# Half of the bonus moved to GpSimd, and the experts' up matmuls widened to 464 columns with the second sum added behind them

## The chip, the cores and the metric

The kernel runs on one core of a Trainium2 chip. The metric is the device time of one execution in microseconds (us), as the median of several runs; less is better. Engines are named as in the profile: PE is TensorE (matmuls; PEld its weight loads), DVE is VectorE, ACT is ScalarE, POOL is GpSimd, SP is SyncE, which issues most DMAs.

## The reference

Two stages follow each other. The first is a linear attention with decay over 4 batches, 8 heads, 768 positions and 48 dimensions:

```python
for t in range(S):
    cur = np.einsum('bhd,bhe->bhde', u[None] * kt, vt)
    y[:, :, t] = np.einsum('bhd,bhde->bhe', rt, state + cur)
    state = w[None, :, :, None] * state + np.einsum('bhd,bhe->bhde', kt, vt)
```

The term with `u` is called the bonus here: position t sees its own key and value with the weight u. The second stage takes the 3072 rows of 384 numbers as tokens. A token whose `x @ w_skip` is positive goes to the one of 8 experts with the largest gate logit and gets

```python
h = np.maximum(xc[mask] @ w1[e], 0.0)
y[mask] = gate_w[mask, None] * (h @ w2[e])
```

added to itself; w1 is 384 x 1024 and w2 1024 x 384 for each expert. All is float32.

## The kernel before

**Attention.** The positions are cut into chunks of 64, and two batches are worked at a time, so there are NT = 24 steps. A step on TensorE is: the scores of the next chunk (L446), the part that comes from the state (`across`, L532), transposes of k (L459) and of an earlier output (L575), the state's update (L479) and the part within the chunk (`within`, L508), which needs the masked scores. VectorE masks the scores from PSUM with two COPY_PREDICATED (L467, L468); the next `within` waits for them. For the chunks to come, VectorE scales r by the decay (`prep_r`, part 0, L416) and multiplies half of the result by u (`prep_r`, part 1, L424: the first BH = 2 of 4 pairs of heads); ScalarE does the other half (`bonus`, L410). Both halves land in the tile `rd`, which the scores read. GpSimd scales k (`prep_k`, L434, tile `kd`). `rd` and `kd` have four buffers each.

The order of the work is written out by hand: each engine runs its instructions in the order of the program, and the loop over n (L893 to L936) lays them down. In step n come the scores, masks and `across` of chunk n + 1, the bonus half of chunk n + 2 on ScalarE, the transpose of k for n + 2, k for n + 3 on GpSimd, a slice of the routing on VectorE (`tick`, how many slices by the table DEAL), then `prep_r` of n + 3 in two parts with the state's update between them. From step 7 on, in twelve steps (LOADS with LEAD), GpSimd also splits a piece of expert 0's weights (L116), after ScalarE has rounded it (L115). Routing begins at step 8.

**Experts.** The kernel splits each float32 operand of the experts in a high part, rounded to the type float32r, and the rest. ScalarE makes the high part (`hi`, `xh`, `hh`), VectorE or GpSimd the low one (`lo`, `xl`, `hl`), and a product is the sum of three matmuls: high by high, high by low, low by high. Each expert has two tiles of tokens, 128 and 104 of CAP = 232. Experts 1 to 7 go through `expert`; expert 0, and expert 1's beginning, are interleaved by the string PLAN with `single`, which works on one tile of 128 tokens. For each of the 8 blocks of 128 features, `up` issues 9 matmuls of 232 columns: three chunks of w1 by (high by xh, high by xl, low by xh), each with a weight load of its own. Two blocks share one PSUM bank (464 columns), and `rectify` takes both at once: ScalarE writes hh = max(ph, 0), VectorE writes hl = max(ph, 0) − hh, both from PSUM. Four banks take turns. Then, per pair of blocks, two pieces of the next expert's weights are split (`split_next(2)`). There are 12 pieces of 128 x 512 an expert; those with j % 3 == 2 go to GpSimd (j % 6 == 2 for expert 2's pieces), the others to VectorE. Each split frees a buffer for the load of a piece of the expert after; NST2 = 14 buffers hold pieces on their way. After the ups, the next expert's tokens are transposed (`turn`), and the downs of the two tiles follow (L170, 24 matmuls of 384 columns each), which read hh and hl block by block. VectorE adds the result to the token (`mix`, L175) when a tile's downs are through, and GpSimd scatters it (L178).

At the start of expert 2 VectorE has six small checks (L1069 to L1075) ahead of its first rectify, at that of expert 3 six more (L1081 to L1086). Expert 7 has no weights to split.

Of the kernel before, what the change touches and what calls it, by code (L numbers as in the profile page):

```python
# [22 lines left out]
P = 128  # L23
# [7 lines left out]
CAP = 232  # L31
# [16 lines left out]
PLAN = "aaasBsaBBxBasBxsgaBBgusBgsBguBBgBs"  # L48
NPC = 12
NST = 4  # L50
NST2 = 14
LEAD = 3
LOADS = [4, 5, 6, 8, 9, 10, 12, 13, 14, 16, 17, 18, 19, 20, 21]
W_MIN, W_MAX = 0.8, 1.2
# [7 lines left out]
def tile_wkv_moe(  # L62
# [89 lines left out]
        nc.scalar.copy(xh, pt)  # L152
        nc.vector.tensor_tensor(xl, pt, xh.bitcast(F32), ALU.subtract)

    def up(ph, w1, f, xh, xl):
        fs = slice(f * P, (f + 1) * P)
        k = 0
        for c in range(NCC):
            for a, b in ((w1[0], xh), (w1[0], xl), (w1[1], xh)):
                nc.tensor.matmul(ph, a[:, c, fs], b[:, c, :], start=(k == 0), stop=(k == 3 * NCC - 1))  # L160
                k += 1

    def rectify(ph, hh, hl):
        nc.scalar.activation(hh, ph, AF.Relu)  # L164
        nc.vector.scalar_tensor_tensor(hl, ph, 0.0, hh.bitcast(F32), ALU.max, ALU.subtract)

    def down(py, w2, f, hh, hl):
        k = 3 * f
# [81 lines left out]
    with ExitStack() as actx:  # L250
# [158 lines left out]
                rd = rds[n][:, hp]  # L409
                nc.scalar.mul(rd[:, :, 1], rd[:, :, 0], uw[:, hp : hp + 1])  # L410

        def prep_r(n, parts=(0, 1)):
            d = loaded[n][0]
            if 0 in parts:
                rds[n] = wk.tile([DR, NHP, 2, 2, C], F32, tag="rd", name=f"rd{n}", bufs=4)
                nc.vector.tensor_tensor(  # L416
                    rds[n][:, :, :, 0],
                    d[:, 0],
                    w_d[:, n % NSUB, 0][:, :, None].to_broadcast([DR, NHP, 2, C]),
                    ALU.mult,  # L420
                )
            if 1 in parts:
                rd = rds[n]
                nc.vector.tensor_tensor(  # L424
                    rd[:, :BH, :, 1],
                    rd[:, :BH, :, 0],
                    uw[:, :BH, None, None].to_broadcast([DR, BH, 2, C]),
                    ALU.mult,
                )
# [463 lines left out]
        for n in range(NT - 1):  # L893
            if n + 5 < NT:
                load_dm(n + 5)
            if n + 4 < NT and n:
                load_v(n + 4)
            if n in LOADS:
                piece(LOADS.index(n))
            scores(n + 1)  # L900
            mask_scores(n + 1)
            across(n + 1)
            if n - LEAD in LOADS[:NPC]:
                piece(LOADS.index(n - LEAD), split=True)
            elif n == NT - 2:
                piece(NPC, split=True)
            if 0 < n and n + 2 < NT:
                bonus(n + 2, BH)
            turn_k(n + 2)
            if 0 < n <= TE and n % GB == 0:  # L910
                gate_back(n - 1)
            turn_x(n)
            if n + 3 < NT:
                prep_k(n + 3)
            for kind in (1, 2, 4):
                step_route(kind)
            tick(DEAL.get(n, 0))
            if n + 3 < NT:
                prep_r(n + 3, (0,))
            back = state(n + 1)  # L920
            if n + 3 < NT:
                prep_r(n + 3, (1,))
            if n == NT - 2:
                gate_some(n, NT - 1 - TE)
                while next(mid) == 0:
                    pass
            within(n + 1, kcopy.get(n + 2, xcopy[n]))
            evac(n + 1)
            if n < TE and n % GB == GB - 1:
                gate_some(n)  # L930
            if back:
                back()
            if n + 1 in ends:
                routes.append([route(ends[n + 1], n + 1), 0, n + 1])
            if 1 <= n < 5:
                next(setup, None)  # L936
# [31 lines left out]
    with ExitStack() as mctx:  # L968
# [12 lines left out]
        def splitter(e, skip=0):  # L981
            pieces = iter(range(skip, NPC) if e < E else ())

            def split_next(k):
                for _ in range(k):
                    j = next(pieces, None)
                    if j is not None:
                        split_piece(e, j, nc.gpsimd if j % (6 if e == 2 else 3) == 2 else nc.vector)
                        if e > 1:
                            load_next(1)  # L990

# [3 lines left out]

        def turn_one(e, j):
            if j == 0:
                turned[e] = tuple(
                    w2pool.tile([P, NCC, CAP], F32R, tag="x" + t, name=f"x{t}{e}") for t in ("h", "l")
                )  # L1000
            xh, xl = turned[e]
            c = TILES[j][1]
            turn(bank("pt")[:, :DM].rearrange("p (c q) -> p c q", q=P), j * E + e, xh[:, :, c], xl[:, :, c])

        def turn_all(e):
            for j in range(NJ):
                turn_one(e, j)

        def expert(e, xh, xl):
            w1, w2 = views(e)  # L1010
            split_more = splitter(e + 1)

# [6 lines left out]
            hh = w2pool.tile([P, NFC, CAP], F32R, tag="hh", name=f"hh{e}")  # L1019
            hl = w2pool.tile([P, NFC, CAP], F32R, tag="hl", name=f"hl{e}")  # L1020
            for f0 in range(0, NFC, 2):
                ph = bank("ph")[:, : 2 * CAP].rearrange("p (i q) -> p i q", q=CAP)
                for i in range(2):
                    up(ph[:, i, :], w1, f0 + i, xh, xl)
                rectify(ph, hh[:, f0 : f0 + 2, :], hl[:, f0 : f0 + 2, :])
                yield
                split_next(2)
            if e + 1 < E:
# [17 lines left out]
        for c in PLAN:  # L1046
# [8 lines left out]
            elif c == "s":  # L1055
                split_next(1)
            elif c == "u":
                opened = opened or expert(1, *turned.pop(1))
                next(opened)
            elif c == "g":  # L1060
                gather(next(rest), w2pool)
# [3 lines left out]
        for e in range(1, E):  # L1065
# [10 lines left out]
            if e == 3:  # L1076
# [7 lines left out]
                nc.vector.tensor_tensor(lmin[:, 0:1], redo, cnt[:, 2:3], ALU.add)  # L1084
                nc.vector.tensor_scalar(lmin[:, 0:1], lmin[:, 0:1], 1.0, None, ALU.min)
                nc.vector.tensor_copy(flags[:, 1:2], lmin[:, 0:1])  # L1086
            both(opened if e == 1 else expert(e, *turned.pop(e)))


    any_v = nc.values_load(flags[0:1, 1:2], min_val=0, max_val=1)  # L1090
# [231 lines left out]
```

## Time and profile before

| what | us |
|---|---|
| median of 3 runs | 268.32 |
| the runs | 268.32, 272.85, 266.75 |
| the profiled execution | 267.35 |
| its span | 265.7 |
| busy: TensorE, VectorE, ScalarE, GpSimd | 249.5, 187.3, 139.5, 130.9 |

The profile is of one execution. Its span runs from the first to the last instruction; the execution's own time is 1.65 us longer. The stages follow each other: attention to about 118 us, expert 0 and the beginning of expert 1 to 147 us, the experts from there to 259 us, with expert 2 beginning at 157 us. Where a view gives rows with two numbers, the first is the start in us from the span's start and the second the duration. In rows that group instructions, the number behind the bar is their busy time in us, then the mean of one in ns, then the idle time of the engine before them and what ended it. The clock of TensorE was 0.993 of full speed on average.

### The profile page before, as it was taken

To read this page: it belongs to the slowest core of one execution; us is meant where nothing else is said; L and a number is where in the kernel's file an instruction comes from. 1 tells how busy PE (TensorE), PEld (TensorE's weight loads), DVE (VectorE), ACT (ScalarE), POOL (GpSimd) and SP (SyncE) were. 2 spreads that over 40 slices of the span, in tenths; PEclk is the share of its full clock that TensorE was granted. 3 is DMA by queue.
4 is the path that set the end of the run, shared out by engine and by line. 5 is a ranking of instruction groups with operands and counts; after the bars stand their busy time and mean duration, and the time that the engine had idled before them with its cause. 6 is when DMAs were issued, how large, how long until landed. Compare 5 with 4: busy or idle time off the path is not lost.

```text
span 265.7 us, 8819 instructions
## 1 busy us (share of the span) xinstructions
PE 249.5 (94%) x3593; PEld 229.1 (86%) x3594; DVE 187.3 (70%) x364; ACT 139.5 (53%) x314; POOL 130.9 (49%) x130
## 2 busy tenths in 40 slices
PE   7899888989999999899999999999999999999990
PEld 2689777877988989778799899999999999999990
DVE  7997446588989989786466996988478385692300
ACT  2556555656757667445377706648176282670200
POOL 8666233353728625502878837455535445345011
PEclk9999999999999999999999999999999999999997
DMA  6968788988899886449599797777738566001000
GB/s 196 292 191 265 210 239 266 275 273 266 246 260 280 238 276 179 104 119 317 164 326 277 248 323 259 219 233 243 251 110 259 171 205 218 20 1 46 0 35 21
DMA packets 31137, 53.92 MB, mean 203 GB/s; under 512 B 4603, under 2 KB 14471, under 8 KB 31088
## 3 DMA queue, kind: packets, MB, share of 16 engines
q1 hardware_dynamic: 28896, 48.09, 60.0%
q0 software_dynamic: 2048, 5.18, 6.2%
q8 instruction: 30, 0.49, 0.8%
q14 instruction: 19, 0.16, 0.2%
q10 hardware_dynamic: 144, 0.00, 0.0%
HBM read 45.46 MB, written 8.39 MB: 203 GB/s over the span
## 4 chain that ended last, share of the span: by engine, by line
PE 71%; DVE 18%; DMA 4%; issue 3%; ACT 1%; SPq 0%; POOL 0%; POOLq 0%; DVEq 0%
PE ps_p L170 11%; PE ps_y L170 11%; PE ps_p L446 6%; PE ps_p L160 5%; PE ps_r L160 5%; PE ps_l L160 5%; PE ps_y L160 5%; PE ps_y L508 5%; DVE am L467 3%; PE ps_s L479 3%; DVE am L468 3%; DVE rd L416 2%; PE ps_l L459 2%; DVE rd L424 2%; PE ps_y L532 2%
## 5 line engine op out<-in xcount | busy, mean ns | idle before, releaser
L116 POOL TENSOR_TENSOR lo<-raw,hi 128x512 fp32r<-128x512 f32 x40 | 54.1, 1355 | 59.7 <-ACT hi L115 48.6
L115 ACT CAST hi<-raw 128x512 fp32r<-128x512 f32 x96 | 54.7, 623 | 0.0
L116 DVE TENSOR_TENSOR lo<-raw,hi 128x512 fp32r<-128x512 f32 x56 | 50.7, 930 | 2.5 <-ACT hi L115 1.9
L434 POOL TENSOR_TENSOR kd<-dm,w_d 128x512 f32<-128x512 f32 x23 | 31.6, 1382 | 15.4 <-DMA dm<-in_dm_dram 8.3
L178 POOL DMA_INDIRECT out_dram<-xg,sid x16 | 17.3, 1079 | 36.3 <-DVE xg L175 28.5
L467 DVE COPY_PREDICATED am<-below,ps_p 128x512 f32<-128x512 int8 x24 | 17.7, 738 | 17.6 <-PE ps_p L446 17.5
L446 PE MATMUL ps_p<-rd,kd 64*64 64x128 f32 x768 | 27.3, 276 | 0.8 <-issue 0.8
L128 POOL DMA_INDIRECT xg<-out_dram,gid x16 | 18.4, 1151 | 16.8 <-DMA raw<-in_w_dram 10.8
L446 PEld LDWEIGHTS ps_p<-rd,kd 64*64 64x64 f32 x768 | 21.0, 132 | 4.5 <-issue 2.4
L508 PE MATMUL ps_y<-vz,am 128*64 128x96 f32 x384 | 20.6, 248 | 3.9 <-DVE am L468 1.6
L164 ACT ACTIVATE hh<-ps_p 128x464 fp32r<-128x464 f32 x7 | 3.9, 559 | 37.6 <-PE ps_p L160 22.9
L410 ACT ACTIVATE rd<-rd,uw 128x128 f32<-128x128 f32 x50 | 17.2, 395 | 9.6 <-DVE rd L416 9.6
L508 PEld LDWEIGHTS ps_y<-vz,am 128*64 128x64 f32 x384 | 17.4, 137 | 5.2 <-ACT xT L576 1.9
L479 PE MATMUL ps_s<-vz,kt 128*64 128x96 f32 x352 | 19.6, 252 | 0.9 <-issue 0.9
L461 ACT COPY kt<-ps_l 128x512 f32<-128x512 f32 x22 | 12.9, 585 | 13.0 <-PE ps_l L459 12.8
L170 PE MATMUL ps_p<-hi,hh 128*128 128x384 f32 x56 | 19.4, 347 | 0.0
L170 PE MATMUL ps_p<-hi,hl 128*128 128x384 f32 x56 | 19.0, 340 | 0.4 <-issue 0.4
L479 PEld LDWEIGHTS ps_s<-vz,kt 128*64 128x64 f32 x352 | 15.3, 136 | 4.3 <-issue 4.2
L170 PE MATMUL ps_y<-hi,hh 128*104 128x384 f32 x56 | 18.9, 338 | 0.0
L170 PE MATMUL ps_y<-lo,hh 128*104 128x384 f32 x56 | 18.9, 337 | 0.0
L170 PE MATMUL ps_y<-hi,hl 128*104 128x384 f32 x56 | 18.9, 337 | 0.0
L170 PE MATMUL ps_p<-lo,hh 128*128 128x384 f32 x56 | 18.8, 336 | 0.0
(239 smaller groups left out, 670.3 us busy)
## 6 DMA issues: line engine op xcount, KB each, us to landing
raw<-in_w_dram SPq DMA_DIRECT2D x96, 256.0 KB
dm<-in_dm_dram SPq DMA_DIRECT2D x24, 512.0 KB
vz<-in_tok_dram SPq DMA_DIRECT2D x48, 96.0 KB
out_dram<-xt SPq DMA_DIRECT2D x48, 96.0 KB
out_dram<-xt SPq DMA_DIRECT2D x4, 192.0 KB
xg<-out_dram,gid POOLq DMA_INDIRECT x16
out_dram<-xg,sid POOLq DMA_INDIRECT x16
wgp<-in_wgq_dram SPq DMA_DIRECT2D x1, 96.0 KB
```

The costliest lines, as they stand in the source:

```text
L115: nc.scalar.copy(hi, t)
L116: eng.tensor_tensor(lo, t, hi.bitcast(F32), ALU.subtract)
L128: ins = nc.gpsimd.indirect_dma_start(out=xg[:m], out_offset=None, in_=out[0:rows], in_offset=bass.IndirectOffsetOnAxis(ap=gid[:m, q : q + ...
L160: nc.tensor.matmul(ph, a[:, c, fs], b[:, c, :], start=(k == 0), stop=(k == 3 * NCC - 1))
L170: nc.tensor.matmul(py, a, b[:, f, :], start=(k == 0), stop=(k == 3 * NFC - 1))
L178: ins = nc.gpsimd.indirect_dma_start(out=out, out_offset=bass.IndirectOffsetOnAxis(ap=sid[: listed(q), q : q + 1], axis=0), in_=xs.pop(q)[ ...
L410: nc.scalar.mul(rd[:, :, 1], rd[:, :, 0], uw[:, hp : hp + 1])
L434: (eng or nc.gpsimd).tensor_tensor(kds[n], d[:, 1], w_d[:, n % NSUB, 1][:, :, None].to_broadcast([DR, NHP, 2, C]), ALU.mult,)
L446: nc.tensor.matmul(ps_p[q * C : (q + 1) * C, a, 2 * hp * C : 2 * (hp + 1) * C], kd[h, hp, q, :], rd[h, hp, q].rearrange("p s c -> p (s c)" ...
L467: nc.vector.copy_predicated(shape(am[n % 2]), below, p[:, :, 0])
L479: nc.tensor.matmul(s[a * C : (a + 1) * C, :, hp * D : (hp + 1) * D], kt[:, hp, a, :], t[:, :, a, hp, :], start=i == 0 and hp == 0, stop=Tr ...
L508: ins = nc.tensor.matmul(place_y(a, c)[:, :, g, :], am[n % 2][:, a, hp * C : (hp + 1) * C], t[:, :, a, hp, :], start=g == 0 and n % NSTEP ...
```

## The change

There are four edits.

1. The second part of `prep_r`, 128 x 256, is done by GpSimd in place of VectorE for chunks 3 to 23. It stands at the beginning of step n for chunk n + 2, ahead of the split and the kd of that step; before, it stood at the end of step n − 1.
2. xh and xl of an expert lie side by side in one tile x. `up` issues, per chunk of w1, one matmul of 464 columns (the high weights by xh and xl) and one of 232 (the low weights by xh, added to the first half). The sum that came from xl thus stands apart in the bank's second half, and a bank now holds one block of features in place of two.
3. `rectify` runs once per block: ScalarE copies the second half from PSUM to a tile h (three buffers), VectorE adds the first half, ScalarE makes hh from h, VectorE hl from h and hh.
4. NST2 is 12 in place of 14, and of expert 2's pieces those with j % 4 == 2 go to GpSimd: three in place of two.

```diff
-NST2 = 14
+NST2 = 12
...
-    def up(ph, w1, f, xh, xl):
+    def up(ph, w1, f, x):
         fs = slice(f * P, (f + 1) * P)
-        k = 0
         for c in range(NCC):
-            for a, b in ((w1[0], xh), (w1[0], xl), (w1[1], xh)):
-                nc.tensor.matmul(ph, a[:, c, fs], b[:, c, :], start=(k == 0), stop=(k == 3 * NCC - 1))
-                k += 1
-
-    def rectify(ph, hh, hl):
-        nc.scalar.activation(hh, ph, AF.Relu)
-        nc.vector.scalar_tensor_tensor(hl, ph, 0.0, hh.bitcast(F32), ALU.max, ALU.subtract)
+            nc.tensor.matmul(
+                ph.rearrange("p s q -> p (s q)"),
+                w1[0][:, c, fs],
+                x[:, c].rearrange("p s q -> p (s q)"),
+                start=(c == 0),
+                stop=(c == NCC - 1),
+                skip_group_check=True,
+            )
+            nc.tensor.matmul(
+                ph[:, 0, :], w1[1][:, c, fs], x[:, c, 0, :], start=False, stop=(c == NCC - 1), skip_group_check=True
+            )
+
+    def rectify(ph, h, hh, hl):
+        nc.scalar.copy(h, ph[:, 1, :])
+        nc.vector.tensor_tensor(h, ph[:, 0, :], h, ALU.add)
+        nc.scalar.activation(hh, h, AF.Relu)
+        nc.vector.scalar_tensor_tensor(hl, h, 0.0, hh.bitcast(F32), ALU.max, ALU.subtract)
...
-        def prep_r(n, parts=(0, 1)):
+        def prep_r(n, parts=(0, 1), eng=None):
...
-                nc.vector.tensor_tensor(
+                (eng or nc.vector).tensor_tensor(
                     rd[:, :BH, :, 1],
...
+            if 0 < n < NT - 2:
+                prep_r(n + 2, (1,), nc.gpsimd)
             scores(n + 1)
...
             back = state(n + 1)
-            if n + 3 < NT:
-                prep_r(n + 3, (1,))
...
-                        split_piece(e, j, nc.gpsimd if j % (6 if e == 2 else 3) == 2 else nc.vector)
+                        split_piece(e, j, nc.gpsimd if j % (4 if e == 2 else 3) == 2 else nc.vector)
...
-                turned[e] = tuple(
-                    w2pool.tile([P, NCC, CAP], F32R, tag="x" + t, name=f"x{t}{e}") for t in ("h", "l")
-                )
+                turned[e] = w2pool.tile([P, NCC, 2, CAP], F32R, tag="x", name=f"x{e}")
...
-                ph = bank("ph")[:, : 2 * CAP].rearrange("p (i q) -> p i q", q=CAP)
-                for i in range(2):
-                    up(ph[:, i, :], w1, f0 + i, xh, xl)
-                rectify(ph, hh[:, f0 : f0 + 2, :], hl[:, f0 : f0 + 2, :])
+                for f in (f0, f0 + 1):
+                    ph = bank("ph")[:, : 2 * CAP].rearrange("p (s q) -> p s q", q=CAP)
+                    up(ph, w1, f, x)
+                    h = w2pool.tile([P, CAP], F32, tag="h", name=f"h{e}_{f}", bufs=3)
+                    rectify(ph, h, hh[:, f, :], hl[:, f, :])
                 yield
                 split_next(2)
```

How this moves instructions is read from the order of each engine's instructions in the two programs. On ScalarE, at the beginning of an expert whose successor's weights are split (`raw` numbers are pieces), there stood before

```order
L164 ACTIVATE hh_3659<-ps_p 128x464
L115 CAST hi_87<-raw_0_3455 128x512
L115 CAST hi_87<-raw_1_3459 128x512
L164 ACTIVATE hh_3659<-ps_r 128x464
L115 CAST hi_87<-raw_2_3489 128x512
L115 CAST hi_87<-raw_3_3493 128x512
```

and now stands

```order
L171 COPY h_0_3496<-ps_p 128x232
L173 ACTIVATE hh_3488<-h_0_3496 128x232
L171 COPY h_1_3507<-ps_r 128x232
L173 ACTIVATE hh_3488<-h_1_3507 128x232
L115 CAST hi_86<-raw_0_3309 128x512
L115 CAST hi_86<-raw_1_3313 128x512
L171 COPY h_2_3526<-ps_l 128x232
```

One operation on two blocks became four on one block each, and every second one of them (L173) reads what VectorE has written.

On VectorE, at the same place, there stood

```order
L165 SCALAR_TENSOR_TENSOR hl_3660<-ps_p,hh_3659 128x464
L116 TENSOR_TENSOR lo_89<-raw_0_3455,hi_87 128x512
L116 TENSOR_TENSOR lo_89<-raw_1_3459,hi_87 128x512
L165 SCALAR_TENSOR_TENSOR hl_3660<-ps_r,hh_3659 128x464
L116 TENSOR_TENSOR lo_89<-raw_3_3493,hi_87 128x512
```

and now stands

```order
L174 SCALAR_TENSOR_TENSOR hl_3489<-h_0_3496,hh_3488 128x232
L172 TENSOR_TENSOR h_1_3507<-ps_r,h_1_3507 128x232
L174 SCALAR_TENSOR_TENSOR hl_3489<-h_1_3507,hh_3488 128x232
L116 TENSOR_TENSOR lo_88<-raw_0_3309,hi_86 128x512
L116 TENSOR_TENSOR lo_88<-raw_1_3313,hi_86 128x512
L172 TENSOR_TENSOR h_2_3526<-ps_l,h_2_3526 128x232
```

The add of a block (L172) now stands behind the splits of the pair before, and the remainder (L174) reads two tiles of SBUF where it read PSUM and SBUF.

On GpSimd, in the steps that make k for chunks 11 to 13, there stood (`kd` with its `dm`, and a split)

```order
L116 TENSOR_TENSOR lo_88<-raw_1_706,hi_86 128x512
L434 TENSOR_TENSOR kd_1009<-dm_781,w_d 128x512
L116 TENSOR_TENSOR lo_88<-raw_2_785,hi_86 128x512
L434 TENSOR_TENSOR kd_1092<-dm_861,w_d 128x512
L434 TENSOR_TENSOR kd_1178<-dm_953,w_d 128x512
```

and now stands

```order
L433 TENSOR_TENSOR rd_915<-rd_915,uw 128x4x64
L116 TENSOR_TENSOR lo_88<-raw_1_705,hi_86 128x512
L443 TENSOR_TENSOR kd_1009<-dm_780,w_d 128x512
L433 TENSOR_TENSOR rd_1020<-rd_1020,uw 128x4x64
L116 TENSOR_TENSOR lo_88<-raw_2_784,hi_86 128x512
L443 TENSOR_TENSOR kd_1092<-dm_860,w_d 128x512
L433 TENSOR_TENSOR rd_1102<-rd_1102,uw 128x4x64
L443 TENSOR_TENSOR kd_1178<-dm_952,w_d 128x512
```

Between any two of the kd there is now a bonus half, which reads what VectorE wrote to `rd` late in the step before; two kd no longer follow each other directly.

More of the change, by code (lines that the diff above doesn't have):

```diff
@@ L997, in turn_one @@
             if j == 0:
-                turned[e] = tuple(
-                    w2pool.tile([P, NCC, CAP], F32R, tag="x" + t, name=f"x{t}{e}") for t in ("h", "l")
-                )
-            xh, xl = turned[e]
+                turned[e] = w2pool.tile([P, NCC, 2, CAP], F32R, tag="x", name=f"x{e}")
+            x = turned[e]
             c = TILES[j][1]
-            turn(bank("pt")[:, :DM].rearrange("p (c q) -> p c q", q=P), j * E + e, xh[:, :, c], xl[:, :, c])
+            turn(bank("pt")[:, :DM].rearrange("p (c q) -> p c q", q=P), j * E + e, x[:, :, 0, c], x[:, :, 1, c])
         def turn_all(e):
@@ L1007, in turn_all, with expert @@
                 turn_one(e, j)
-        def expert(e, xh, xl):
+        def expert(e, x):
             w1, w2 = views(e)
@@ L1057, in tile_wkv_moe @@
             elif c == "u":
-                opened = opened or expert(1, *turned.pop(1))
+                opened = opened or expert(1, turned.pop(1))
                 next(opened)
@@ L1086, in tile_wkv_moe @@
                 nc.vector.tensor_copy(flags[:, 1:2], lmin[:, 0:1])
-            both(opened if e == 1 else expert(e, *turned.pop(e)))
+            both(opened if e == 1 else expert(e, turned.pop(e)))
     any_v = nc.values_load(flags[0:1, 1:2], min_val=0, max_val=1)
```

## The prediction

> **What bounds the kernel now.** I read the page first: its span line and the shares of the chain that ended last.
>
> ```profile
> span 265.7 us, 8819 instructions
> ...
> PE 71%; DVE 18%; DMA 4%; issue 3%; ACT 1%; SPq 0%; POOL 0%; POOLq 0%; DVEq 0%
> ```
>
> TensorE carries the chain, VectorE a fifth of it. Where each does shows in the busy times of three stretches: the attention steps in which routing runs, experts 2 to 6, and expert 7, which splits no weights.
>
> ```profile
> core 0: us, PE busy (x) PEld busy (x) DVE busy (x) ACT busy (x) POOL busy (x), PEclk, DMA share, GB/s
> 53.00:110.00 57.00, 54.00 (x1372) 48.12 (x1364) 52.43 (x101) 37.40 (x93) 29.98 (x22) 1.00 0.82 243
> 157.00:242.50 85.50, 85.50 (x634) 84.46 (x633) 59.94 (x94) 45.75 (x91) 41.87 (x33) 1.00 0.57 181
> 242.50:259.70 17.20, 16.44 (x120) 15.93 (x119) 4.42 (x7) 2.24 (x4) 2.02 (x2) 1.00 0.07 20
> ```
>
> In the first stretch VectorE is busy 52.4 of 57 us. In the second TensorE never rests. Its VectorE has 25.6 us left over, 5.1 an expert; ScalarE has 8 an expert. The chain of waits, in order of time, shows one expert:
>
> ```profile
> 191.28 2.01 PE ps_p L160 x18
> 193.29 2.02 PE ps_r L160 x18
> ...
> 197.32 2.01 PE ps_y L160 x18
> 199.93 4.22 PE ps_p L170 x24
> 204.14 4.20 PE ps_y L170 x24
> 208.35 2.01 PE ps_p L160 x18
> ```
>
> Eighteen ups take 2.01, 0.112 each; 24 downs 4.20, 0.175 each; an expert 208.35 − 191.28 = 17.07. Nothing but TensorE sets this stage now, so whatever the change adds to ScalarE and VectorE is free only while it stays hidden.
>
> **Part one: the ups.** A block of 128 features costs nine matmuls of 232 columns, 9 × 0.112 = 1.005. It becomes three of 464 and three of 232. The trace has no 464; the bounds are 384 columns at 0.175 and the 512 columns of the single tiles:
>
> ```profile
> 133.19 1.39 PE ps_y L200 x6
> ```
>
> That is 0.232 each, and on the line between the two 464 columns take 0.210. A block then takes 3 × 0.210 + 3 × 0.112 = 0.966: 0.039 less, 0.31 an expert, **−2.2 us** over seven experts if nothing else intervenes. The bounds are 0 (464 columns cost two halves of 0.112) and 2.7 (0.208, on the line through 232 and 384 columns).
>
> [...]
>
> **Part two: the bonus.** Twenty-one instructions L424 leave VectorE; those on the chain in the routing steps are
>
> ```profile
> 70.52 0.42 DVE rd L424
> 75.42 0.42 DVE rd L424
> 84.38 1.38 DVE rd L424
> 89.11 0.42 DVE rd L424
> 93.92 0.42 DVE rd L424
> 95.92 0.88 PE ps_y L508 x16
> 96.80 1.08 PE ps_p L446 x32
> 102.19 0.42 DVE rd L424
> 107.20 1.38 DVE rd L424
> ```
>
> The next mask starts at each one's end. A mask otherwise waits for L508 and L446, 0.88 + 1.08 = 2.0 after the mask before; at these seven places TensorE had done that, so the step shortens: 5 × 0.35 (0.42 less what neighbours on VectorE overlap) + 2 × 1.31 = 4.4. Elsewhere, and in all steps before 53 us, VectorE waits for TensorE and nothing is won: that is the lower bound, 0. A second gain hides in GpSimd's order. It can now not start the kd of a step before the bonus, which waits for VectorE's L416. In the timelines of VectorE and GpSimd:
>
> ```profile
> 56.47 1.29 POOL L434 TENSOR_TENSOR kd<-dm,w_d 128x512 f32<-128x512 f32 x1 [0.23 <-DMA dm<-in_dm_dram]
> ...
> 56.62 1.22 DVE L665 TENSOR_TENSOR oh<-eq,m 128x64 bf16<-128x64 f32 x1
> ...
> 88.25 0.23 DVE L665 TENSOR_TENSOR oh<-eq,m 128x64 bf16<-128x64 f32 x1
> ```
>
> The same L665 takes 0.23 alone and 1.22 while a kd that ran ahead holds it up. The kd's last 0.5 us can still meet later routing, so of three such meetings (about 1 us each) I count half, 1.5. Sum **−5.9**, between 0 and 4.4 + 3 = 7.4. GpSimd pays between 0.65 (half of 1.29) and 1.29 a step for it; I take 0.70, the work being half. Behind it in GpSimd's queue stand a split and the kd, which TensorE wants a step later; with 1.3 each a step fills 3.3 of 4 to 5 us, so this is covered. Were it not, the scores would wait 0.7 a step, 15 us in all. SP's queue keeps its order; two fewer raw buffers leave twelve pieces in flight, one whole expert (17 us) ahead of use: nothing.
>
> **Part three: the second sum.** Per block ScalarE and VectorE now hand over three times: copy, add, relu, remainder. All four are 232 wide, and the nearest rows by form are
>
> ```profile
> L612 ACT COPY lt<-ps_l 128x128 f32<-128x128 f32 x6 | 1.6, 267 | 2.7 <-PE ps_l L603 2.7
> ...
> L152 ACT CAST xh<-ps_s 128x312 fp32r<-128x312 f32 x4 | 1.7, 432 | 0.0
> ...
> L153 DVE TENSOR_TENSOR xl<-ps_s,xh 128x312 fp32r<-128x312 f32 x4 | 1.9, 475 | 0.0
> ...
> L410 ACT ACTIVATE rd<-rd,uw 128x128 f32<-128x128 f32 x50 | 17.2, 395 | 9.6 <-DVE rd L416 9.6
> ...
> L115 ACT CAST hi<-raw 128x512 fp32r<-128x512 f32 x96 | 54.7, 623 | 0.0
> ```
> ```profile
> 158.56 0.38 DVE L1070 SCALAR_TENSOR_TENSOR lok<-lg,lok 128x216 f32<-128x216 f32 x1
> ```
>
> Copy 0.36, between 0.267 and 0.432. Add 0.39, below 0.475. Relu from SBUF 0.40, between 0.395 and 0.46 on the line to 0.623. Remainder 0.39, from 0.38. A pair of blocks on ScalarE alone, with hand-overs of 0.035 and successive operations overlapping by 0.10, is 2 × (0.36 + 0.39 + 0.40) + hand-overs and overlaps + two casts at 0.52, in all 3.3 us. TensorE makes a pair in 1.93. From the first block's end at 1.0, three pairs and the 2.4 to the last relu make 13.3, and the last remainder ends 13.7 us after the expert's first up. The downs of block 7 would start at 7.73 + 0.60 (transposes) + 7 × 0.525 = 12.0. Cover gone: TensorE waits.
>
> VectorE adds its own delay, shown in the timelines of both engines:
>
> ```profile
> 196.50 1.29 POOL L116 TENSOR_TENSOR lo<-raw,hi 128x512 fp32r<-128x512 f32 x1 [3.24 <-ACT hi L115]
> ...
> 195.94 0.64 DVE L165 SCALAR_TENSOR_TENSOR hl<-ps_r,hh 128x464 fp32r<-128x464 f32 x1
> 196.96 1.38 DVE L116 TENSOR_TENSOR lo<-raw,hi 128x512 fp32r<-128x512 f32 x1 [0.38 <-ACT hi L115]
> 198.26 0.63 DVE L165 SCALAR_TENSOR_TENSOR hl<-ps_l,hh 128x464 fp32r<-128x464 f32 x1
> 198.81 0.68 DVE L116 TENSOR_TENSOR lo<-raw,hi 128x512 fp32r<-128x512 f32 x1
> ```
>
> A split on VectorE takes 0.68 alone and 1.38 beside GpSimd's; it ends just behind GpSimd's. L165, one input from PSUM, keeps 0.63 to 0.64. The new remainder reads both inputs from SBUF, so it can be held up as the split is. Each engine in its order, these durations and this one wait give for the old kernel the second and third L165 at 4.65 and 6.99 after the first up (rows: 4.66, 6.98) and an expert of 17.04 (17.07). For the new one, in us after the first up:
>
> | pair | first copy | first add | last relu ends | casts end |
> |---|---|---|---|---|
> | 0 | 1.0 | 1.4 | 3.4 | 4.4 |
> | 1 | 4.3 | 5.1, behind two splits | 7.1 | 8.2 |
> | 2 | 8.1 | 9.5, behind split 3, held by GpSimd | 11.5 | 12.5 |
> | 3 | 12.4 | 12.8 | 15.0 | – |
>
> The last remainder ends at 15.4, its down 0.2 later, the second tile 4.2 after that: 19.8 an expert, **+2.8** each for experts 2 to 6, 14.0. [...] Without that wait the layout gives 18.85, +1.8.
>
> Three experts differ. Expert 2 has the checks ahead of its first add, expert 3 those of the counts; expert 1 waits already:
>
> ```profile
> 151.16 0.63 DVE L165 SCALAR_TENSOR_TENSOR hl<-ps_y,hh 128x464 fp32r<-128x464 f32 x1
> 159.48 0.16 DVE L1075 CAST bad<-lmin 128x1 bf16<-128x1 f32 x1
> 176.50 0.15 DVE L1086 CAST flags<-lmin 128x1 int32<-128x1 f32 x1
> ```
> ```profile
> 151.84 0.97 PE ps_p L170 x4
> ```
>
> Experts 2 and 3 begin at 157.0 and 174.1, so their first adds come at 2.7 and 2.5 instead of 1.4: 1.3 and 1.1 more. In expert 1 the remainder that ends at 151.79 becomes the last of four blocks at 2.3 a pair plus two splits, about 155.5: +2.9. Expert 7 splits nothing; its chain of 1.15 a block ends at 10.7, before 12.0, and it keeps its −0.3. **Sum of part three with the ups in it:** 14.0 + 2.4 + 2.9 − 0.3 = +19.0.
>
> **Total.** The profiled execution took 267.35 with its 265.7 of span: 267.35 + 19.0 − 5.9 = 280.5. It lies 0.97 below the median of 268.32 (266.75 to 272.85); I forecast **281.0 us**, for the median.
>
> **Bounds.** With all four operations at their lowest rows (0.27 to 0.29) and the wait, an expert is 18.05, +1.0; without the wait TensorE hides everything. At the highest (0.43, 0.475, 0.46, 0.42) it is 21.1, +4.1.
>
> **Rivals.** *Hidden after all* (the other side): the four operations run as short as their 128-wide rows and rarely meet GpSimd; then only the gains stay, 267.35 − 2.2 − 4.4 = 260.8. For it: 5.1 us an expert are free on VectorE. Against it: the sum of work is not the matter, the alternation on two in-order engines is. Faster than 2% (below 263) 0.07. *Half hidden*: short operations with the wait, 267.35 + 6 × 1.0 + 2.4 − 0.3 − 5.9 = 269.6; within 2% 0.14. The loads giving nothing is inside these: 2.2 us. *The bonus backfires* by holding VectorE's two-input work, 0.7 in each of 21 steps, 15 us on top: 295.5. Against it: it starts when L416 ends, under the two masks, which read PSUM and stay at 0.74 beside GpSimd. 0.03, within the slower. *The chain of the second sum decides*, as forecast: slower 0.79 with the backfire. It decides once the last remainder is later than 12.0 us after the first up.
>
> The range is 269 to 290: the half-hidden case below, the highest rows for about half of the experts above. Two per cent, 5.4 us, is about what a measurement of this kernel can tell from no change.
>
> **What would show it.** Eighteen ups' worth of columns in about 1.93; L171 to L174 near 0.36, 0.39, 0.40, 0.39; TensorE idle 2 to 4 us in each first down tile of experts 1 to 6, ended by ScalarE or VectorE, none in expert 7; experts 19 to 20.5 apart; attention ending 4 to 7 us sooner. A TensorE without gaps after 157 us would prove me wrong.

## The result and the profile after

The changed kernel takes 291.38 us in the median of its four runs (288.35, 289.77, 293.0 and 480.98), the kernel before on the same chip 270.59 in the median of four (266.75, 268.32, 272.85 and 1356.81). The ratio is taken over the two fastest runs of each, which alone count as undisturbed; it is 1.0805, 95% interval 1.0627 to 1.0983: **8% slower**. Slower was forecast, at 0.79; the forecast of 281.0 was too low and its range, 269 to 290, ended below the median. The profiled execution took 288.35, 21.0 more than the one before.

The page of the changed kernel shows what took TensorE's place on the chain that ended last (before: PE 71, DVE 18, DMA 4, ACT 1):

```profile
span 286.5 us, 8700 instructions
...
PE 55%; DVE 16%; DMA 10%; ACT 9%; issue 5%; SPq 2%; POOL 1%; POOLq 0%; ACTq 0%; DVEq 0%
```

ScalarE and DMA have grown on it. Busy times of stretches of the changed kernel (columns: stretch, length, busy time of PE, weight loads, DVE, ACT, POOL, then granted clock, DMA share, GB/s) show the routing part of attention, two steady experts and expert 7:

```profile
53.00:110.00 57.00, 53.98 (x1362) 47.74 (x1354) 45.94 (x90) 36.40 (x89) 40.79 (x35) 1.00 0.85 253
...
201.90:222.00 20.10, 18.15 (x105) 15.95 (x103) 14.52 (x29) 12.14 (x30) 7.44 (x7) 1.00 0.56 171
222.00:242.00 20.00, 18.07 (x103) 15.88 (x102) 14.44 (x29) 12.19 (x30) 7.35 (x7) 1.00 0.56 173
...
262.00:278.20 16.20, 16.15 (x97) 15.08 (x95) 7.11 (x20) 5.21 (x16) 4.38 (x4) 1.00 0.10 33
```

A steady expert takes 20.0 instead of 17.07, with no engine busy all the time; expert 7, which splits nothing, takes 16.1 and TensorE does not pause in it. In the 20.0 the second sum's engines wait for each other. The chain of the changed kernel, in order of time, through one of these experts (first up at 221.96):

```profile
229.04 1.13 ACT hi L115 x2
...
230.20 1.35 DVE lo L116
231.55 0.32 DVE h L172
...
231.89 0.41 ACT hh L173
...
232.32 0.40 DVE hl L174
232.72 0.32 DVE h L172
...
233.37 1.13 ACT hi L115 x2
234.50 0.25 ACT h L171
...
235.21 0.41 ACT hh L173
...
235.64 0.48 DVE hl L174
236.12 0.32 DVE h L172
...
236.46 0.41 ACT hh L173
...
236.91 0.88 PE ps_p L179 x3
237.79 4.19 PE ps_y L179 x24
```

Read it downwards as a shuttle: two casts on ScalarE, the split of the second on VectorE (1.35 beside GpSimd's, where 0.68 is its time alone), then add, relu and remainder of one block and of the next, crossing from engine to engine at every step. TensorE gets the last block's relu at 236.87, 14.9 us after the first up, and could have used it at about 12.0 by the prediction's reckoning of its ups and downs.

From the start of one expert's last mix to the next (VectorE's timeline) the whole span comes apart as follows. Expert 1 is counted from its first up; "predicted" is the prediction's own term.

| stretch | before | after | difference | predicted |
|---|---|---|---|---|
| start to expert 1's first up | 134.42 | 131.33 | −3.1 | −5.9 |
| expert 1 | 23.32 | 26.74 | +3.4 | +2.9 |
| expert 2 | 16.38 | 23.58 | +7.2 | +4.1 |
| expert 3 | 17.20 | 20.36 | +3.2 | +3.9 |
| experts 4, 5, 6 | 51.20 | 60.09 | +8.9 | +8.4 |
| expert 7 | 16.46 | 16.09 | −0.4 | −0.3 |
| last mix to the end | 6.67 | 8.27 | +1.6 | 0 |
| span | 265.65 | 286.46 | +20.8 | +13.1 |

### The profile page after: what moved, and what is told of

It reads as the page before. It is cut to its first block, busy times and chain, and to the rows that moved or that the text cites. A ratio compares the mean times of both kernels' runs of the same rounds, so it can differ in the third digit from the quotient of the medians.

```text
span 286.5 us, 8700 instructions
## 1 busy us (share of the span) xinstructions
PE 256.5 (90%) x3425; PEld 224.5 (78%) x3426; DVE 197.6 (69%) x426; ACT 160.8 (56%) x398; POOL 146.2 (51%) x152
## 4 chain that ended last, share of the span: by engine, by line
PE 55%; DVE 16%; DMA 10%; ACT 9%; issue 5%; SPq 2%; POOL 1%; POOLq 0%; ACTq 0%; DVEq 0%
PE ps_y L179 9%; PE ps_p L455 6%; DVE lo L116 5%; DMA dm<-in_dm_dram 5%; ACT hi L115 5%; PE ps_s L488 5%; PE ps_y L517 4%; DVE h L172 3%; PE ps_p L179 3%; PE ps_l L468 3%; DMA raw<-in_w_dram 3%; PE ps_l L158 3%; PE ps_y L541 3%; PE ps_p L158 3%; ACT hh L173 2%
## 5 line engine op out<-in xcount | busy, mean ns | idle before, releaser
L116 DVE TENSOR_TENSOR lo<-raw,hi 128x512 fp32r<-128x512 f32 x55 | 45.2, 845 | 6.4 <-ACT hi L115 4.0
L173 ACT ACTIVATE hh<-h 128x232 fp32r<-128x232 f32 x56 | 22.3, 398 | 40.7 <-DVE h L172 38.0
L174 DVE SCALAR_TENSOR_TENSOR hl<-h,hh 128x232 fp32r<-128x232 f32 x56 | 24.1, 431 | 26.0 <-ACT hh L173 23.2
L443 POOL TENSOR_TENSOR kd<-dm,w_d 128x512 f32<-128x512 f32 x23 | 34.0, 1477 | 10.2 <-DMA dm<-in_dm_dram 6.2
L179 PE MATMUL ps_p<-hi,hh 128*128 128x384 f32 x56 | 21.1, 377 | 11.4 <-DVE h L172 7.1
L455 PE MATMUL ps_p<-rd,kd 64*64 64x128 f32 x768 | 26.5, 275 | 0.0
L179 PEld LDWEIGHTS ps_p<-hi,hh 128*128 128x128 f32 x56 | 10.6, 189 | 15.9 <-DVE h L172 8.0
L433 POOL TENSOR_TENSOR rd<-rd,uw 128x256 f32<-128x256 f32 x21 | 12.8, 612 | 17.6 <-DVE rd L425 8.7
L425 DVE TENSOR_TENSOR rd<-dm,w_d 128x512 f32<-128x512 f32 x24 | 19.7, 820 | 2.8 <-DMA dm<-in_dm_dram 2.7
L179 PE MATMUL ps_p<-hi,hl 128*128 128x384 f32 x56 | 20.2, 360 | 0.0
L470 ACT COPY kt<-ps_l 128x512 f32<-128x512 f32 x22 | 12.8, 582 | 12.4 <-PE ps_l L468 12.3
```

The lines of the kernel that those rows point to most:

```text
L116: eng.tensor_tensor(lo, t, hi.bitcast(F32), ALU.subtract)
L173: nc.scalar.activation(hh, h, AF.Relu)
L174: nc.vector.scalar_tensor_tensor(hl, h, 0.0, hh.bitcast(F32), ALU.max, ALU.subtract)
L179: nc.tensor.matmul(py, a, b[:, f, :], start=(k == 0), stop=(k == 3 * NFC - 1))
L425: nc.vector.tensor_tensor(rds[n][:, :, :, 0], d[:, 0], w_d[:, n % NSUB, 0][:, :, None].to_broadcast([DR, NHP, 2, C]), ALU.mult,)
L443: (eng or nc.gpsimd).tensor_tensor(kds[n], d[:, 1], w_d[:, n % NSUB, 1][:, :, None].to_broadcast([DR, NHP, 2, C]), ALU.mult,)
```

## The experiments

Steady experts (4 to 6) are compared by their period, which repeats within 0.1 us in every profile; whole times of one kernel differ by about 3% between runs. The ratios stand against the kernel before, with 95% intervals.

### The order of the four operations

**Two blocks at a time** (`pair_order`):

```
-                    rectify(ph, h, hh[:, f, :], hl[:, f, :])
+                    pair.append((ph, h, hh[:, f, :], hl[:, f, :]))
+                rectify(pair)   # copy, copy, add, add, relu, relu, remainder, remainder
```

> The changed kernel with one thing altered: the operations of two blocks are issued as copy, copy, add, add, relu, relu, remainder, remainder instead of one block after the other. Work, sizes, engines and buffers are the same. Theory (the alternation of two in-order engines sets an expert: while one block's add, relu and remainder go to and fro, the next block's copy stands behind them): laid out with the durations that the changed kernel's profile has (0.355, 0.395, 0.405, 0.40) an expert falls from 20.0 to 17.4, so five steady experts give back 13 and experts 1 and 2 some 2 to 6 more: 269 to 274 in a profiled execution. Rival (the added work on VectorE and ScalarE, and GpSimd holding VectorE, set it): the same 20.0 and the same time within 2 us.

Ratio 1.0331 (1.0205 to 1.0457), profiled 274.13. In the stretches of this kernel one steady expert is:

```profile
212.60:230.20 17.60, 17.02 (x103) 16.09 (x102) 14.28 (x28) 11.92 (x30) 7.44 (x7) 1.00 0.62 198
```

and its chain holds TensorE but for one place, where a split on VectorE runs beside GpSimd's:

```profile
219.11 0.62 ACT hi L115
219.75 1.36 DVE lo L116
221.11 0.32 DVE h L174
221.48 4.49 PE ps_p L183 x24
225.96 4.20 PE ps_y L183 x24
```

The busy times of ScalarE, VectorE and GpSimd are those of the changed kernel to 0.3 us, and 2.4 of the 3.0 us lost in a steady expert are back. So most of the loss is not the amount of the work; it is that add, relu and remainder of one block stand in the queue of two in-order engines ahead of the next block's copy and add. With two blocks side by side one engine works on the second while the other has the first.

**Splits moved, order left** (`block_spread`) asks the opposite: are the splits between the blocks the trouble?

```
-                split_next(2)                      # behind each pair of blocks
+                split_next(2 if e == 1 else 1)
...
-                split_next(2)                      # in each down tile
+                split_next(2 if e == 1 else 4)
```

> The changed kernel, one block after the other as it is, with only the splits of experts 2 to 6 dealt 1, 1, 1, 1, 4, 4. Theory (the order copy, add, relu, remainder block by block is the loss, not the splits between): steady experts stay near 19.8, as the layout gives, against 20.03. Rival (the splits in the queue are the loss): about 17.

A steady expert takes 19.75, the one execution timed 287.39. Taking half of the splits from behind the pairs gives back 0.3 of 3.0 as long as the blocks go one by one. The test is not quite clean: the last relu does end 1.0 sooner after the first up, but 0.7 of that is lost at the start of the next expert, where TensorE waits 0.5 until a mix that now stands behind splits on VectorE. The splits are thus worth between 0.3 and 1.0 here, and as the main cause the rival falls.

**GpSimd's hold** (`pair_vector`) is the pairwise kernel with the later splits all on VectorE:

```
-                        split_piece(e, j, nc.gpsimd if j % (4 if e == 2 else 3) == 2 else nc.vector)
+                        split_piece(e, j, nc.vector)
```

> The kernel with pairwise order, and in it all weight splits of experts 2 to 7 on VectorE, none on GpSimd: VectorE gets four more splits an expert (2.7 us), and nothing of two SBUF inputs runs beside GpSimd. Theory (with the alternation gone, what is left of the loss is GpSimd holding VectorE): an expert falls from the 17.60 measured with pairwise order to 17.0, as the layout gives; five steady experts 3 less, about 271 in a profiled execution. Rival (VectorE's amount of work sets it): the 2.7 us more an expert make it longer than 17.6. Of the span's end: if it is the number of GpSimd's instructions that lengthens the last 6.7 us to 8.4, this kernel, which has fewer than the kernel before, ends in 6.7 though its bonus is on GpSimd.

The period is 17.25, the ratio 0.9991 (0.992 to 1.0061). Four more splits on VectorE made an expert 0.35 shorter, since VectorE's own splits now take their 0.68 instead of 1.35. The theory gave 17.0; it overstated the gain by 0.25, but the sign rules out the rival. The end of the span is 6.7 us again, as in the kernel before.

**Both** (`pair_spread`) takes the pairwise order, the splits on VectorE and the dealing of `block_spread`:

> Pairwise order with all later splits on VectorE, and in experts 2 to 6 the twelve splits of the next weights dealt 1, 1, 1, 1 behind the pairs of blocks and 4, 4 in the two down tiles, instead of 2 each time. Same work. Theory (what is left of the loss with pairwise order is the splits that stand in the two in-order queues ahead of the last pair's operations): the last remainder ends 10.6 us after the first up instead of 12.4, before TensorE wants it, and an expert falls from the 17.25 measured to 16.7, below the 17.07 of the kernel before: 264 to 266 in a profiled execution, 1 to 2 per cent below the kernel before. Rival (ScalarE and VectorE are simply short of time): 17.2 again, the wait only moves to the next expert's weights.

```profile
206.90:223.70 16.80, 16.80 (x104) 16.07 (x103) 15.02 (x34) 11.93 (x30) 4.05 (x3) 1.00 0.64 206
```

TensorE is busy for all of the 16.8 us: the wide ups have their gain, 0.30 an expert, and the second sum costs nothing. Ratio 0.9978 (0.9935 to 1.0021), profiled 264.41. The same dealing was worth 0.3 block by block and 0.5 here (17.25 to 16.77), where no wait of TensorE is left. The whole is no faster than the bonus edit alone (below): from the first up to the last mix it takes 123.8 against 124.6, since experts 1 and 2 together take 41.1 instead of 39.7 and give most of the gain back.

### The two halves of the change

**The second sum without the bonus edit** (`sum_alone`):

```
-            if 0 < n < NT - 2:
-                prep_r(n + 2, (1,), nc.gpsimd)
...
+            if n + 3 < NT:
+                prep_r(n + 3, (1,))
```

> The changed kernel with the whole bonus back on VectorE at its old place: wide ups and the second sum alone. Theory (the second sum costs everything that is lost, and the bonus wins 3.1): 3 us slower than the changed kernel, about 291.5 in a profiled execution, 24 above the kernel before; experts 4 to 6 are 20.03 apart as in the changed kernel. Rival (the bonus on GpSimd disturbs the first experts, so that part of the loss in experts 1 and 2 is its doing): less than 18 above the kernel before.

Ratio 1.076 (1.0624 to 1.0896), profiled 289.12, 21.8 above the profiled kernel before; steady experts 20.05. From the first up to the last mix this kernel takes 146.1, the changed kernel 146.9, and the 0.8 lies in experts 2 and 3. So the bonus on GpSimd has hardly a part in the experts' loss; 24 was too much, because the bonus brings less than 3 net.

**Wide ups without the second sum** (`no_second_sum`):

```
-        nc.scalar.copy(h, ph[:, 1, :])
-        nc.vector.tensor_tensor(h, ph[:, 0, :], h, ALU.add)
-        nc.scalar.activation(hh, h, AF.Relu)
-        nc.vector.scalar_tensor_tensor(hl, h, 0.0, hh.bitcast(F32), ALU.max, ALU.subtract)
+        nc.scalar.activation(hh, ph[:, 0, :], AF.Relu)
+        nc.vector.scalar_tensor_tensor(hl, ph[:, 0, :], 0.0, hh.bitcast(F32), ALU.max, ALU.subtract)
```

> The changed kernel without copy and add: relu and remainder read the first half of each block's columns from PSUM as in the kernel before, one block at a time. It leaves out the products of the high weights with the low parts of x from the result; the matmuls are all still made. Theory (wide ups are worth 0.31 an expert by themselves, and only the second sum costs): experts 16.7 apart and TensorE without gaps from 157 us on, 267.35 - 2.2 - 3.1 = 262 in a profiled execution. First rival (halving the blocks, eight evacuations for four, already costs): experts over 17.1 apart, time no better than the 264 of the bonus alone. [...]

A steady expert takes 16.77, TensorE busy throughout; profiled 264.48 where theory had 262, and ratio 0.9993 (0.9942 to 1.0043). The steady gain is the predicted 0.3. It does not add up to 2.2: from expert 1's first up to the last mix this kernel takes 124.25, the bonus edit alone 124.55. Experts 1 and 2 take 24.0 and 17.1 instead of 23.3 and 16.4, so most of what experts 3 to 7 gain is given back there. In its waits TensorE lost 0.9 us twice in that part, both times until VectorE's remainder ended. That eight evacuations for four fit worse between the single tiles' work would explain it, but was not tested.

**The bonus edit alone**, measured twice (the diff is the reverse of the one for `sum_alone`, on the kernel before):

> The kernel before with the bonus edit alone: half of the bonus on GpSimd as the first operation of a step; ups, remainders and raw buffers as before. Theory (the bonus is worth what the changed kernel shows, and the DMA of the decays takes the rest of the 5.9 that was predicted): expert 1 starts about 3.1 us earlier than in the kernel before (131.5 instead of 134.6 us into the span), experts 2 to 6 stay 17.07 apart, time 3 us shorter: 264 against the 267.35 of the profiled execution. First rival (the sum of the prediction): 5.9 shorter, 261.5. Second rival (the 3.1 came from something else than the bonus): no change.

> The kernel with the bonus edit alone once more, in five rounds on the chip of the rearranged kernel, since three left 0.974 to 1.002. If the bonus is worth 3.3 us in the attention stage and loses 1.7 at the end, as the profiles have it, the ratio is 0.994; by the difference of the medians measured first it is 0.988. The rearranged wide ups are better than this only if their ratio is lower by more than the intervals.

Ratios 0.9883 (0.9744 to 1.0022) and 0.9967 (0.9921 to 1.0013): by the closer one 0.3% faster, which is not told from no change; the profiled executions took 265.84 and 266.22 where theory had 264. No kernel here beats the one before by more than its interval. Expert 1's first up is at 131.07 and 131.56. Over all profiles with the bonus on GpSimd it lies between 130.03 and 132.86 (nine, mean 131.8), over those without between 133.18 and 137.62 (five, mean 134.9): the edit is worth 3.1 at that point. The profiles bound it poorly, since before the routing TensorE has pauses that nothing in the trace releases, and they differ from execution to execution.

What replaces the bonus on the chain stands in the chain of `bonus_alone`:

```profile
55.57 1.45 SPq L277
...
58.32 4.01 DMA raw<-in_w_dram
...
62.35 0.62 ACT hi L115
...
65.00 5.06 DMA dm<-in_dm_dram
...
70.22 1.83 POOL kd L434
```

From 55 to 72 us the chain runs from SP's queue to a weight load, to a load of `dm` (a chunk's r and k; the expectations call it the DMA of the decays), to a kd that takes 1.83. The median kd takes 1.31 in the kernel before and 1.32 in the changed one, but seven of 23 take over 1.6 in the changed kernel and two in the kernel before; here those at 43.68 and 52.91 take 1.76 and 1.80. In the changed kernel, too, the chain has a load of `dm` of 5.1 us at 48.7 and one of 5.4 at 56.7. Whether the loads would still bind if the weights came later was not tried.

### Three smaller suspects

**Two raw buffers fewer** (`twelve_raws`, `NST2 = 12` in the kernel before):

> The kernel before with 12 instead of 14 raw buffers. Theory (they cost nothing, as predicted): experts 2 to 6 stay 17.07 apart and expert 1 to the end of expert 2 stays 39.5 us. Rival (late weight loads are part of the 10.6 us that experts 1 and 2 lost): that stretch grows by 1 us or more.

Experts 2 and 3 take 16.37 and 17.20, as before; expert 1 with expert 2 takes 39.7 (before 39.7). For the kernel before, the term of nothing was right; in the changed kernel a weight load stands on the chain of expert 2 (below), so there it is not shown. The 271.01 of its one execution comes from the attention stage: expert 1 starts at 137.62, the latest of all profiles.

**The half clock.** In the changed kernel the granted clock falls twice while TensorE has work. The stretches on either side of each fall, 3.41 us long, and one in a steady expert for comparison:

```profile
137.59:141.00 3.41, 1.23 (x7) 0.94 (x7) 2.35 (x6) 1.72 (x6) 2.60 (x3) 0.99 0.94 309
141.00:144.41 3.41, 3.41 (x13) 3.30 (x12) 0.83 (x2) 2.54 (x5) 3.10 (x3) 0.51 0.77 256
171.72:175.13 3.41, 1.85 (x7) 0.97 (x6) 2.27 (x6) 2.34 (x7) 1.27 (x1) 0.99 0.72 231
175.13:178.55 3.42, 3.41 (x11) 3.17 (x12) 3.21 (x6) 3.42 (x8) 1.14 (x1) 0.51 0.62 190
229.75:233.16 3.41, 2.09 (x15) 1.89 (x14) 2.37 (x4) 1.39 (x5) 1.25 (x1) 1.00 0.30 90
```

Behind a stretch with only seven matmuls TensorE works at 0.51, and the next stretch holds 11 to 13 of them. Behind the steady expert's stretch, with 15, the clock stays. `sum_alone` has two such falls, `block_spread` and `fillers` one each, in expert 1, and the pairwise kernels none (mean clock 0.993 to 0.994, in the kernel before 0.993).

In expert 2 of the changed kernel the half clock is only one of two losses. Its chain:

```profile
157.05 4.46 DMA raw<-in_w_dram
...
166.70 1.78 DVE lo L116
168.47 0.32 DVE h L172
...
168.82 0.41 ACT hh L173
...
169.25 1.73 DVE hl L174
...
175.14 1.33 PE ps_p L179 x3
176.47 5.14 PE ps_y L179 x24
```

A weight load that lands at 161.5 stands on it. Counted between first ups, expert 2 takes 23.8 and a steady expert 20.0. A remainder (L174) takes 1.73 beside GpSimd's split, where each of the 32 in experts 3 to 6 takes 0.40 to 0.48, and the last relu ends 17.4 after the first up instead of 15.1, at 175.1, where the clock has only just fallen. The last three downs of the first tile and the 24 of the second then take 1.33 and 5.14 instead of 0.88 and 4.19, together 1.4 more.

**Filling TensorE's pauses** (`fillers`):

```
+                if a is hh and q == E and parts == (0,):
+                    for _ in range(9):
+                        nc.tensor.matmul(y, zeros, ones[:, :DM], start=False, stop=False)
...
+                    for _ in range(8 if e == 2 and j == 0 and f == 6 else 0):
+                        nc.tensor.matmul(py, zeros[:, :m], ones[:, :DM], start=False, stop=False)
```

> The changed kernel with 17 extra matmuls that add zeros to an open sum (384 columns, bf16, 0.16 each): 9 in expert 1 where TensorE waited 2.2 us at 137.9, 8 in expert 2 where it waited 1.3 us at 172.5. Theory (the granted clock falls to 0.50 for 3.41 us after each stretch of 3.41 us in which TensorE had little to do, as in the changed kernel at 141.0 and 175.1, and each costs up to 1.7): with the stretches filled the clock stays at 1.00 through experts 1 and 2 and the kernel with more work is 1.7 to 3.4 us shorter, 285 to 286.7 in a profiled execution. Rival (the half clock has another cause, such as the weights' DMA at 0.9 of its engines in these stretches): the 0.50 stretches stay and the time is the same or up to 2.7 longer.

The 0.16 agrees with rows of the kernel before: bf16 matmuls of 8 columns take 0.166 (L699) and of 512 columns 0.379 at the fastest (L260), on that line 0.42 ns a column, an estimate of 0.16 for 384. In the run the nine of expert 1 take 3.04 together, at a granted clock of 0.50.

```profile
137.25:140.67 3.42, 1.30 (x9) 1.04 (x8) 2.95 (x7) 1.74 (x5) 2.81 (x3) 1.00 0.83 248
140.67:144.08 3.41, 3.37 (x11) 1.99 (x11) 0.40 (x1) 3.39 (x7) 2.89 (x3) 0.50 0.81 274
...
172.00:175.41 3.41, 3.41 (x20) 2.42 (x18) 2.26 (x5) 2.35 (x7) 1.27 (x1) 1.00 0.84 278
175.41:178.82 3.41, 3.11 (x18) 2.76 (x18) 2.81 (x6) 3.41 (x8) 0.74 (x1) 1.00 0.54 173
```

In expert 2 the forecast came: with the pause filled the clock stays at 1.00, at a DMA share of 0.84 (0.72 in the changed kernel), and expert 2 takes 21.27 instead of 23.58. That the fillers did this is not shown beyond doubt: expert 2 begins 1.6 us later here, so it lies otherwise to the 3.41 us stretches, and `block_spread`, without fillers, has no fall in expert 2 either (20.87, and 21.51 in expert 3). Nor is all of the 2.3 the clock's: the last relu ends 16.4 after the first up instead of 17.4, and in the changed kernel the clock fell only at that relu's end. The other 1.4 are the downs at full clock. In expert 1 the attempt failed: the nine fillers stood behind the same wait (2.2 us, until VectorE's add) that they were to fill, the half clock came, and they lengthened expert 1 by 1.0. And of the 2.3 won in expert 2, expert 3 gives 1.35 back (21.71 for 20.36), with VectorE and ScalarE on the chain up to its downs but for one block's ups; that in the changed kernel they work off their backlog while TensorE runs slowly is the likely reason, but is not shown. From the first up to the last mix the two kernels take the same, 146.9; the profiled execution took 289.25 where theory had 285 to 286.7, and the ratio is 1.0894 (1.0731 to 1.1056). So by estimate a half clock costs up to 1.7 where it falls (half of 3.41), in expert 2 it cost 1.4, and filling the pauses won nothing for the whole.

**The end of the span** is longer by 1.6 in the changed kernel and in every kernel with as many GpSimd instructions. Memsets of one column at the places of the bonus, in the kernel before:

```
+            if 0 < n < NT - 2:
+                nc.gpsimd.memset(idle, 0.0)        # more_dummies: three times
```

> The kernel before, its bonus on VectorE, with 21 memsets of one column on GpSimd at the places where the change puts the bonus. Theory (21 more GpSimd instructions move the blocks in which its code is loaded, so that one more load falls behind the last mix): 8.4 us from the start of the last mix to the end of the span, as in all four profiles with the bonus on GpSimd, instead of 6.7. Rival (the bonus itself does it): 6.7. In the attention stage nothing changes; it gives a second profile of attention without the bonus edit.

> The kernel before with 63 memsets of one column on GpSimd instead of the 21 that left the end at 6.7 us. Theory (the number of instruction words on GpSimd decides, and a bonus with its waits takes more than a memset): 8.4 us from the start of the last mix to the end of the span. Rival (something else in the bonus edit lengthens the end): 6.7.

From the start of the last mix to the end: 6.7 with 21 memsets (266.33), 8.5 with 63 (269.62). The queues in that last stretch, first of the kernel with 21 and then of that with 63:

```profile
q14 instruction: 3, 0.02, 1.1%
```

```profile
q14 instruction: 4, 0.03, 1.3%
```

The kernel before (6.7, three loads) and the changed kernel (8.3, four) fit this: it is the number of GpSimd's instructions, not the bonus, and one more load of code falls behind the last mix. The bonus puts more than 21 there, since beside its 21 operations GpSimd's queue has 18 semaphore instructions at their line (L433 of the changed kernel); `pair_vector`, with the bonus but 27 splits fewer, ends in 6.7.

## Why the prediction was right and where it was wrong

**The bound and the steady expert: right.** The layout gave 19.8, measured 20.0. Its table can be laid beside ScalarE's timeline of the changed kernel (the expert starts at 221.96):

```profile
223.00 0.35 ACT L171 COPY h<-ps_p 128x232 f32<-128x232 f32 x1 [2.35 <-DVE xg L184]
...
226.32 0.34 ACT L171 COPY h<-ps_l 128x232 f32<-128x232 f32 x1
...
230.07 0.34 ACT L171 COPY h<-ps_p 128x232 f32<-128x232 f32 x1
...
234.41 0.34 ACT L171 COPY h<-ps_l 128x232 f32<-128x232 f32 x1
...
236.46 0.40 ACT L173 ACTIVATE hh<-h 128x232 fp32r<-128x232 f32 x1 [0.56 <-DVE h L172]
```

The first copies of the pairs come at 1.04, 4.36, 8.11 and 12.45 after the first up (table: 1.0, 4.3, 8.1, 12.4), the last relu ends at 14.9 (15.0). The durations taken, 0.36, 0.39, 0.40 and 0.39, are 0.34, 0.39, 0.40 and 0.41 on average in this expert.

**Part one: right in the row, short in the sum.** The eight blocks of expert 7 take 7.73, from 262.01 to 269.74, which is 8 × 0.966. From start to start a matmul of 464 columns takes 0.21 to 0.22 there and one of 232 takes 0.10 to 0.11; the prediction took 0.210 and 0.112. The 0.3 an expert is there (`no_second_sum`, `pair_spread`), but of the 2.2 over seven experts only 0.3 remained in `no_second_sum`, since experts 1 and 2 gave the rest back.

**Part two: mis-sized; this step failed.** The step "4.4, plus half of three meetings" made −5.9; measured are 3.1 at the first up, and 1.6 of it is lost again at the end of the span. The chain's seven bonus instructions did leave it, but I priced each as if only TensorE stood behind VectorE. One meeting did go: the routing operation that took 1.22 beside a kd takes 0.23 in the changed kernel (at 52.52). In the profiles DMA and GpSimd's kd (1.48 on average, 1.29 in the row that I used) stand on the chain instead; that they alone took the missing 2.8 was not shown. That the end of the span could change did not occur in the sum at all. The bonus itself takes 0.612 on GpSimd (0.70 taken) and nobody waits for it, as forecast: the backfire did not come.

**Experts 1 to 3: one of three mis-sized; this step failed too.** Expert 1 was +2.9 forecast and +3.4 measured, expert 3 +3.9 and +3.2. Expert 2 was +4.1 and became +7.2. The step was to let the steady layout start 1.3 later, behind the checks, with every duration kept. Two durations did not hold. A remainder of 0.39 took 1.73 beside GpSimd's split, which the prediction had said could happen but left out of expert 2, whose term is a steady expert's plus 1.3; with it the last relu came 2.3 after a steady expert's instead of 1.3. And in "the second tile 4.2 after that" the 24 downs took 5.14: the granted clock was 0.51 from 175.13 to 178.55, which with the three downs before cost 1.4 in all. These two make 2.4 of the missing 3.1.

**The total.** Against 280.5 for the profiled execution: +2.8 for attention, +3.3 for the experts (22.3 measured, 19.0 summed), +1.6 for the end, 0.2 for what lies around the span, together 288.4, which is the 288.35. The rest to 291.38 is the choice of execution: the profiled one is the fastest of the four runs, and the median of the four counts the run of 480.98 (without it the middle run is 289.77). The forecast's last step also slipped: 280.5 + 0.97 is 281.4, not 281.0. **The range** varied the durations of the four operations alone and held every other term fixed, with a gain of 5.9 that no row bounded from the side of the DMA. Its reason, the highest rows in about half of the experts, gives 280.5 + 3 × 1.3 = 284.4, not 290; that 288.35 and 289.77 still lie under 290 is luck.

The rivals "hidden after all" and "half hidden" fell with TensorE's pauses: it waits in every one of experts 1 to 6 and not in 7, as forecast.

## What to carry to other kernels

In these runs work handed to and fro between two engines, each in its order, was priced by its chain, not by the engines' free time: 5 and 8 free us an expert did not hide 3 us of it, while issuing two blocks side by side gave back 2.4 without removing an instruction. A table that replays each engine's queue in order, with durations from rows of near shapes and the waits seen, forecast the steady stage of five kernels here within 0.3 us; transitions between stages, the start and the end of a kernel need bounds of their own. Before work is taken from the engine on the chain, the price has to be bounded by what stands second there, DMA included.

## What the runs showed of the hardware

**TensorE's clock fell to half while TensorE had work, six times.** In the stretches of 3.41 us before these falls (changed kernel, `sum_alone`, `block_spread`, `fillers`) TensorE had 1.2 to 2.1 us of work, in 7 to 9 matmuls. The timelines show pauses of 2.18 and 1.26 us in the two of the changed kernel, 2.17 in that of `block_spread` (where the 384-column matmuls behind it take 0.52 for 0.34) and 2.16 in that of `fillers`; in the two of `sum_alone` the idle time is 2.18 and 1.34 in all. Stretches of the changed kernel and of `sum_alone` with 1.97 to 2.25 us, in 13 to 15 matmuls, were followed by a clock of 1.00. Busy time alone does not draw the line: in `fillers` the stretch from 123.60 to 127.01 holds 1.67 us of work in 9 matmuls behind a pause of 2.00, and the 512-column matmuls after it keep their 0.39. The threshold stays open. The falls of the changed kernel and of `sum_alone` last 3.41 us and lie 34.13 apart in both, ten times 3.41. In the changed kernel the clock falls a third time at 280.95, behind the last matmul (0.50 to the end of the span), 139.95 after the first, 41 times 3.413.

**GpSimd's instruction count shows at the end.** With 21 memsets three loads of queue q14 lie behind the last mix and the end takes 6.7 us, with 63 four loads and 8.5: one load of code and 1.8 us more. The runs show the extra load, not which engine waited for it.

**Pauses of TensorE without a releaser** of 0.7 to 0.9 us stand at 31, 37 and 43 us of the profile before, and not in that of `sum_alone`, whose TensorE has the same instructions there. Sums from one profile carry that uncertainty.
